# Row maxima of the scores from a 64-row product, two heads side by side, in an attention and feed-forward kernel

## The chip, the cores and the metric

The kernel runs on one core of one Trainium2 chip. The metric is device time in microseconds (us) of one execution; less is better. The kernel before was run three times. Its profile is of one further execution of the same program, recorded by the hardware.

## What is computed

Attention over 8 batches of 12 heads, 448 positions and a head width of 64, and then a feed-forward layer over the 3584 positions. All is in fp32 at the border of the kernel; the weights come as 64-bit floats.

```python
q_n, k_n = rmsnorm(q, g_q), rmsnorm(k, g_k)
scores = (q_n @ k_n.T) / sqrt(64)
scores = scores - max(scores, axis=-1)
attn = exp(scores); attn = attn / (sum(attn, axis=-1) + 1e-9)
x = heads side by side of attn @ v          # 3584 x 768
out = (s * relu(x @ w_in) ** 2 + b) @ w_out   # 768 -> 2048 -> 768
```

The maximum that is subtracted is only a shift: whatever is taken in its place comes out again in the division by the sum, as long as the exponentials neither overflow nor vanish.

## The kernel before

**Two parts.** The first part does the attention and, in its gaps, the first product of the feed-forward layer (`x @ w_in`) of the batch before. The second part does the last batch's first product and then `@ w_out`. Matmul operands are fp32r; where fp32r is not precise enough an operand is split into a high part and the rest, so that a product takes up to three matmuls.

**Pairs and slots.** Heads go in 48 pairs, j = 0 the even one and j = 1 the odd one. The program is a list written out slot by slot: 8 slots for a pair (`W`), one for each of four chunks of keys of each head, and 22 slots ahead of pair 0. Slot s of pair p stands at 8p + s; here "slot 0 to 7 of a pair" is meant. In a slot TensorE gets, in this order:

- `score_t` (L407, L410): two matmuls into the tile `st`, keys on the rows and queries along the columns. The first multiplies `ka` by `qa`, the second adds `kb` by `qb`.
- two matmuls `ph` of the feed-forward product as filling (L182),
- `score` (L369): one matmul into `sh`, with queries on the rows: a quarter of a head's queries (every fourth one, 112 columns of weights) against all 448 keys. It serves the maxima alone,
- two more `ph`, then `weigh` (L466): two or three matmuls `av`, weighting the values, for the slot before the last, and two more `ph`.

The filling starts at slot 60 of the list (`START`), in pair 7. In the first 12 pairs `weigh` is one fp32 matmul instead of the two or three.

**The tiles ka, qa, kb, qb** have 128 rows, 448 columns for each head of a pair, and exist twice (pairs take turns). For each head rows 0 to 63 of `ka` hold the high part of the keys and rows 64 to 127 the rest; `qa` holds the high part of the queries in both halves. So `ka` by `qa` over 128 rows gives k_hi q_hi + k_lo q_hi. `kb` holds the high part of the keys in rows 0 to 63 and a row of ones in row 64, `qb` the rest of the queries in rows 0 to 63 and in row 64 the negated maximum; the other rows are zero. So the exponent's argument is complete when both matmuls are done.

**How a head gets there.** Up to pair 8 (`NR` is 9) the heads come by `load_rows`, `norm_rows`, `turn` and `split_turned`; from pair 9 on by `load_kq`, `spread`, `scale` (POOL L331, VectorE L332, 15 slots ahead of the head's first slot), `split_kq` (ScalarE L350, L351 13 slots ahead, POOL L353, L354 one slot later) and `double_kb` (a DMA of `ka`'s high part to `kb`, 10 slots ahead).

**The maxima.** `score` of a product runs ten slots ahead of its number (`AHEAD`), so one in every slot. `maximum` (VectorE L380) follows in the same slot, and writes a column of `nmx`. When a head's four are there, `shift` (DMA on SP's queue, L357) writes them to the row of `qb`, six slots ahead of the head's first slot.

**Order on the other engines.** In a slot VectorE gets the slot's preparations (`ssq` L311, `scale` L332, `split_x` L516), then `split_e_lo` of the slot before (L447, the low part `al` of the exponentials), then `maximum`, then `convert` and `invert`. ScalarE gets `split_e` of the slot before (L434), `exponent` (L426 or L422), the slot's preparations, and `rectify` (L199). The low part `al` of a slot is thus made one slot later and used by `weigh` two slots later. Engines run in the order that is written; each takes its instructions one after another. `split_x` comes once in 48 slots, in three slots in a row (slots 3, 4 and 5 of a pair), with two VectorE operations each; `ssq` and the odd head's `scale` both fall in slot 5.

**PSUM** has eight banks that are handed out in the order in which they came free (`psum`): a new tile waits until the last reader of the tile before it in that bank is through.

Of the kernel before, what the change touches and what calls it, by code (L numbers as in the profile page):

```python
# [9 lines left out]
F32 = mybir.dt.float32  # L10
# [3 lines left out]
ALU = mybir.AluOpType  # L14
# [11 lines left out]
AHEAD = 10  # L26
# [11 lines left out]
def attention_then_relu2_ffn(  # L38
# [30 lines left out]
    V, S, G, T = nc.vector, nc.scalar, nc.gpsimd, nc.tensor  # L69

    NPAIR, P, _, SEQ = kq.shape
# [4 lines left out]
    D = P // 2  # L76
# [4 lines left out]
    NR = rows0.shape[0]  # L81
    NQ = 4
    QC = SEQ // NQ
# [9 lines left out]
    W = 8  # L93
# [18 lines left out]
    def psum(name):  # L112

        bank = free.pop(0)
        return ps.tile([P, 512], F32, tag=bank, name=name), bank
# [95 lines left out]
    with tc.tile_pool(name="apool", bufs=1) as ap:  # L211
# [40 lines left out]
        def split_turned(p, j):  # L252
            n, a = p % 2, slice(j * SEQ, (j + 1) * SEQ)
            (k, k_bank), (q, q_bank) = (tks.pop((p, j, t)) for t in range(2))
            S.copy(ka[n][:D, a], k)
            S.activation(qa[n][:D, a], q, AF.Copy, scale=gqk[:D])
            S.activation(qa[n][D:, a], q, AF.Copy, scale=gqk[:D])
            yield
            V.tensor_tensor(ka[n][D:, a], k, ka[n][:D, a].bitcast(F32), ALU.subtract)  # L259
            V.scalar_tensor_tensor(  # L260
                qb[n][:D, a], q, gqk[:D], qa[n][:D, a].bitcast(F32), ALU.mult, ALU.subtract
            )
            free.extend((k_bank, q_bank))

# [4 lines left out]
        def warm_up(n):  # L269

            to, bank = psum("warmth")
            for _ in range(n):
                T.matmul(to[:, :P], ident, ident, start=True, stop=True)
            free.append(bank)
# [58 lines left out]

        ka = [ap.tile([P, 2 * SEQ], F32R, name=f"ka{n}") for n in range(2)]
        qa = [ap.tile([P, 2 * SEQ], F32R, name=f"qa{n}") for n in range(2)]
        kb = [ap.tile([P, 2 * SEQ], F32R, name=f"kb{n}") for n in range(2)]
        qb = [ap.tile([P, 2 * SEQ], F32R, name=f"qb{n}") for n in range(2)]
        for t in qb:  # L340
            G.memset(t[D:P].bitcast(F32), 0.0)
        for t in kb:
            G.memset(t[D:P].bitcast(F32), 0.0)
            G.memset(t[D : D + 1].bitcast(F32), 1.0)

        def split_kq(p, j):

            t, n = kqs.pop((p, j)), p % 2
            a = slice(j * SEQ, (j + 1) * SEQ)
            S.copy(ka[n][:, a], t[:, 0])  # L350
            S.copy(qa[n][:, a], t[:, 1])  # L351
            yield
            G.tensor_tensor(ka[n][D:, a], t[D:, 0], ka[n][D:, a].bitcast(F32), ALU.subtract)  # L353
            G.tensor_tensor(qb[n][:D, a], t[:D, 1], qa[n][:D, a].bitcast(F32), ALU.subtract)  # L354

        def move(to, of):
            nc.sync.dma_start(to.bitcast(F32), of.bitcast(F32))  # L357

        def double_kb(p, j):
            a = slice(j * SEQ, (j + 1) * SEQ)  # L360
            move(kb[p % 2][:D, a], ka[p % 2][:D, a])

        def score(i):

            p, c = divmod(i, W)
            j, c = divmod(c, NQ)
            sh, bank = psum(f"sh{i}")
            a = slice(j * SEQ, (j + 1) * SEQ)
            T.matmul(  # L369
                sh[:QC, :SEQ], qa[p % 2][:, a].rearrange("k (p c) -> k c p", c=NQ)[:, c],  # L370
                ka[p % 2][:, a], start=True, stop=True,
            )
            shs[i] = sh, bank

        def maximum(i):
            p, c = divmod(i, W)
            if c == 0:
                nmxs[p] = ap.tile([QC, W], F32R, tag="nmx", bufs=2, name=f"nmx{p}")
            sh, bank = shs.pop(i)
            V.tensor_reduce(  # L380
                out=nmxs[p][:, c : c + 1], in_=sh[:QC, :SEQ], op=ALU.max, axis=AX.X, negate=True
            )
            free.append(bank)

        def shift(p, part):

            to = qb[p % 2][D : D + 1, part * SEQ : (part + 1) * SEQ]
            move(
                to.rearrange("o (p c) -> o p c", c=NQ), nmxs[p][:, part * NQ : (part + 1) * NQ]
            )  # L390
            if part:
                nmxs.pop(p)
# [35 lines left out]
        def split_e(i):  # L428
            p, j, kc, rows = chunk(i)
            if p < NV:  # L430
                return
            ah = ap.tile([P, SEQ], F32R, tag="ah", bufs=3, name=f"ah{i}")
            movers[i] = [ah]
            S.copy(ah[:rows], sts[i][0][:rows, :SEQ])  # L434
# [120 lines left out]
        def filler(n):  # L555

            for _ in islice(fill, n):
                pass
# [4 lines left out]
        def at(s_, f, *a):  # L563
            jobs[s_].append((f, a))

        for p in range(NPAIR):
            s0 = W * p
            if p >= NR:
                at(s0 - 32, load, p)
                at(s0 - 28, norm, p)  # L570
                at(s0 - 24, keep, p)
            for j in range(2):
                s1 = s0 + 4 * j
                if p >= NR:
                    at(s1 - 19, load_kq, p, j)
                    at(s1 - 19, spread, p, j)
                    at(s1 - 15, scale, p, j)
                    at(s1 - 13, split_kq, p, j)
                else:
                    at(max(s1 - 28, FIRST), load_rows, p, j)  # L580
                    at(s1 - 20, norm_rows, p, j)
                    at(s1 - 13, turn, p, j)
                    at(s1 - 12, split_turned, p, j)
                at(s1 - 10, double_kb, p, j)
                at(s1 - 6, shift, p, j)
                at(s1 + 6, take, p, j)
                at(s1 + 7, gather, p, j)
            at(s0 - (9 if p >= NV else 5), load_v, p)
            if p >= NV:
                at(s0 - 3, split_v, p)  # L590
            at(s0 + 13, invert, p)
            at(s0 + 14, divide, p, 1)
            at(s0 + 16, divide, p, 2)
            at(s0 + 18, divide, p, 3)
# [10 lines left out]
        def within(i):  # L605
            return 0 <= i < NSLOT
# [3 lines left out]
        gqk = cpool.tile([P, 1], F32, name="gqk")  # L610
        sb_s = cpool.tile([P, 1], F32, name="sb_s")
        sb_b = cpool.tile([P, 1], F32, name="sb_b")
        with tc.manual_schedule(engines=ORDERED):
            begun = []
            for s_ in range(FIRST, NSLOT + START + 1):
                if s_ == FIRST:
                    nc.sync.dma_start(gg, g_qk)
                    V.scalar_tensor_tensor(gqk, gg[:, 0:1], D**-0.5, gg[:, 1:2], ALU.mult, ALU.mult)
                if s_ == 0:
                    for t, x in ((sb_s, s), (sb_b, b_)):  # L620
                        nc.sync.dma_start(t, x.rearrange("(o d) -> o d", o=1).broadcast_to([P, 1]))
                if s_ == FIRST:
                    warm_up(30)
                if within(s_):
                    score_t(s_)
                filler(FILL[0])
                if within(s_ - 1):
                    split_e(s_ - 1)
                if within(s_):
                    exponent(s_)  # L630
                begun = [g for g in begun if next(g, 0) is None]
                keep_r()
                for f, a in jobs[s_]:
                    if f in late:
                        continue
                    g = f(*a)
                    if g is not None and next(g, 0) is None:
                        begun.append(g)
                ahead = s_ + AHEAD
                scored = within(ahead)  # L640
                if scored:
                    score(ahead)
                filler(FILL[1])
                rectify()
                if within(s_ - 1):
                    split_e_lo(s_ - 1)
                if scored:
                    maximum(ahead)
                for f, a in jobs[s_]:
                    if f in late:  # L650
                        f(*a)
                if within(s_ - 2):
                    weigh(s_ - 2)
                filler(FILL[2])
                b, m = divmod(s_ + 1 - START, W * NP)
                if m == 0 and b > 0:
                    filler(None)
                    units = [(b - 1, fc) for fc in range(NFC)]
                    fill = chain.from_iterable(ffn_in(xs, *u) for u in units) if b < B else iter(())
            rectify()  # L660
            keep_r()
# [146 lines left out]
```

## Time and profile before

| | us |
|---|---|
| median of three runs | 1484.6 |
| lowest and highest of them | 1483.02, 1485.44 |
| the profiled execution | 1483.03 |
| its span, first to last instruction | 1481.2 |
| first scoring matmul `st` starts (slot 0 of pair 0) | 27.0 |
| slot 4 of pair 7 (the filling starts) | 135.5 |
| slot 0 of pair 12 | 232.1 |
| last scoring matmul `st` | 933.1 |

The profiled execution stands 1.57 us under the median of the three runs and inside their spread. 1.83 us of it lie around the span.

How to read what follows. PE is TensorE's matmuls and PEld its weight loads, DVE is VectorE, ACT is ScalarE, POOL is GpSimd, SP the queue of DMA issues. A row of a timeline has the start in us, the duration in us, engine, line, operation, output tile and inputs, shapes, and how many instructions were merged into it (x2: two of them); in brackets idle time of the engine ahead of it and what ended it. For a matmul the shape `128*112 128x448` is rows times columns of the weights, then rows times columns of what streams past. A matmul's duration is modelled to its end, and runs beyond the start of the next one, so what a matmul costs is read from the distance of the starts. A row of windows has the stretch, its length, then for each engine its busy time and number of instructions, then the granted clock, the share of DMA and GB/s.

### The profile page before, as it was taken

The page shows a single profiled execution, that of the slowest core. Times are in us where ns is not written, and L with a number is a line of the kernel's source. Part 1 is how long each engine was busy: PE and PEld are TensorE (multiplying, and loading weights), DVE is VectorE, ACT ScalarE, POOL GpSimd, SP SyncE. Part 2 cuts the span into 40 slices and gives each one's busy share as a digit, 9 for nine tenths or more (in the row PEclk, how much of TensorE's full clock was granted, in tenths as well). Part 3 has the DMA queues.
Part 4 walks back from the last instruction along what each step waited for, and adds up shares of the span by engine and source line. Part 5 has one row for each costly group of instructions (what it writes and reads, how often), then busy time and mean ns, then how long its engine had stood idle before and what let it go on. Part 6 is the DMA issues. An engine that isn't in the chain of part 4 may idle for free. (4 is left out here: it accounts for less than half of the span.)

```text
span 1481.2 us, 21369 instructions
## 1 busy us (share of the span) xinstructions
PE 1443.3 (97%) x7332; PEld 1322.6 (89%) x7332; DVE 862.8 (58%) x1328; ACT 790.5 (53%) x1445; POOL 686.9 (46%) x563
## 2 busy tenths in 40 slices
PE   7998999999999999999999999999999999999998
PEld 6665788899899899899899889999999999999998
DVE  7999996766766666766766664389522222222210
ACT  5777556766766666766766766456322222222210
POOL 7788887777677777777677763100000000000000
PEclk8999999999999999999999999999999999999999
DMA  5456876566666666566666652387333333233200
GB/s 141 130 159 183 233 219 203 171 196 186 188 190 184 189 192 185 170 199 191 188 175 198 189 171 58 118 273 242 105 97 85 96 94 78 79 91 106 79 22 32
DMA packets 218172, 225.31 MB, mean 152 GB/s; under 512 B 77936, under 2 KB 195696, under 8 KB 218064
## 3 DMA queue, kind: packets, MB, share of 16 engines
q1 hardware_dynamic: 218064, 223.95, 51.7%
q8 instruction: 58, 0.95, 0.3%
q14 instruction: 50, 0.41, 0.1%
HBM read 171.71 MB, written 40.82 MB: 143 GB/s over the span
## 5 line engine op out<-in xcount | busy, mean ns | idle before, releaser
L182 PE MATMUL ph<-x,wih 128*128 128x448 f32 x1536 | 490.0, 366 | 1.8 <-DVE x L516 1.8
L182 PEld LDWEIGHTS ph<-x,wih 128*128 128x128 f32 x1536 | 288.7, 188 | 31.7 <-issue 6.4
L380 DVE TENSOR_REDUCE nmx<-sh 112x1 fp32r<-112x448 f32 x384 | 237.0, 620 | 130.7 <-PE sh L369 127.7
L182 PE MATMUL ph<-x,wil 128*128 128x448 f32 x768 | 293.8, 383 | 0.0
L426 ACT ACTIVATE st<-st 128x448 f32<-128x448 f32 (+1 forms) x288 | 151.2, 525 | 220.3 <-PE st L410 213.6
L707 PE MATMUL po<-woh,gh 128*128 128x384 f32 x896 | 228.1, 334 | 0.3 <-ACT r L199 0.3
L707 PE MATMUL po<-wol,gh 128*128 128x384 f32 x896 | 227.9, 334 | 0.0
L707 PE MATMUL po<-woh,gl 128*128 128x384 f32 x896 | 227.7, 334 | 0.0
L466 PE MATMUL av<-ah,vs 128*128 128x448 f32 x576 | 164.3, 366 | 0.1
L369 PE MATMUL sh<-ka,qa 128*112 128x448 f32 x384 | 147.3, 386 | 16.0 <-DVE ka L259 10.9
L707 PEld LDWEIGHTS po<-woh,gh 128*128 128x128 f32 x896 | 161.9, 188 | 0.7 <-ACT r L199 0.6
L707 PEld LDWEIGHTS po<-wol,gh 128*128 128x128 f32 x896 | 161.9, 188 | 0.0
L707 PEld LDWEIGHTS po<-woh,gl 128*128 128x128 f32 x896 | 161.7, 188 | 0.0
L407 PE MATMUL st<-qa,ka 128*128 128x448 f32 (+1 forms) x384 | 159.2, 415 | 1.7 <-ACT e L422 0.8
L182 PEld LDWEIGHTS ph<-x,wil 128*128 128x128 f32 x768 | 144.3, 188 | 17.8 <-issue 6.9
L434 ACT CAST ah<-st 128x448 fp32r<-128x448 f32 (+1 forms) x288 | 153.9, 534 | 1.8
L447 DVE TENSOR_TENSOR al<-st,ah 128x448 fp32r<-128x448 f32 x216 | 132.4, 613 | 35.4 <-ACT ah L434 21.6
L689 ACT ACTIVATE r<-r 128x2048 f32<-128x2048 f32 x28 | 53.7, 1919 | 172.7 <-DMA r<-r_d 172.7
L410 PE MATMUL st<-qb,kb 128*128 128x448 f32 (+1 forms) x384 | 140.2, 365 | 0.0
L690 DVE TENSOR_SCALAR r<-r,sb_s,sb_b 128x2048 f32<-128x2048 f32 x28 | 37.6, 1346 | 173.2 <-ACT r L689 173.2
L507 POOL TENSOR_TENSOR u<-uz,zb 64x448 f32<-64x448 f32 x96 | 115.4, 1203 | 41.4 <-DMA zb<-z_d 27.7
L369 PEld LDWEIGHTS sh<-ka,qa 128*112 128x112 f32 x384 | 107.5, 281 | 28.9 <-ACT wih L138 4.7
(75 smaller groups left out, 2142.1 us busy)
## 6 DMA issues: line engine op xcount, KB each, us to landing
kq<-in_dram SPq DMA_DIRECT2D x78, 448.0 KB, 4.9
rb<-i_d SPq DMA_DIRECT2D x78, 448.0 KB, 5.9
r_d<-r SPq DMA_DIRECT2D x128, 224.0 KB, 2.8
r<-r_d SPq DMA_DIRECT2D x24, 1024.0 KB, 5.9
raw<-in_dram SPq DMA_DIRECT2D x39, 448.0 KB, 5.1
w64i<-in_dram SPq DMA_DIRECT2D x24, 512.0 KB, 4.9
w64o<-in_dram SPq DMA_DIRECT2D x32, 384.0 KB, 4.7
kb<-ka SPq DMA_DIRECT2D x96, 112.0 KB, 3.1
```

Of the source, the lines that this page charges most:

```text
L182: T.matmul(ph[:, :SEQ], w[:, cc, f0 : f0 + P], xs[b, cc][:, part, :], start=n == 0, stop=n == 3 * NCC - 1,)
L369: T.matmul(sh[:QC, :SEQ], qa[p % 2][:, a].rearrange("k (p c) -> k c p", c=NQ)[:, c], ka[p % 2][:, a], start=True, stop=True,)
L380: V.tensor_reduce(out=nmxs[p][:, c : c + 1], in_=sh[:QC, :SEQ], op=ALU.max, axis=AX.X, negate=True)
L407: T.matmul(st[:rows, :SEQ], ka[n][:, keys], qa[n][:, q], start=True, stop=False)
L410: T.matmul(st[:rows, :SEQ], kb[n][:, keys], qb[n][:, q], start=False, stop=True,)
L426: S.activation(st[:rows, :SEQ], st[:rows, :SEQ], AF.Exp)
L434: S.copy(ah[:rows], sts[i][0][:rows, :SEQ])
L447: V.tensor_tensor(al, st[:rows, :SEQ], ah[:rows].bitcast(F32), ALU.subtract)
L466: T.matmul(av[:, :SEQ], x, a, start=kc == 0 and m == 0, stop=kc == 3 and m == len(todo) - 1,)
L507: G.tensor_tensor(u[a], uzs.pop((p, j))[a], zb[a], ALU.mult)
L689: S.activation(r, r, AF.Square)
L707: T.matmul(po[e][0][:, :HALF], x[:, fc, :], w[:, f, e * HALF : (e + 1) * HALF], start=fc == 0 and m == 0, stop=fc == NFC - 1 and m == 2,)
```

## The change

**From pair 9 on `score` uses 64 rows instead of 128**: the high part of the keys by the high part of the queries, without the product of the keys' rest. For the even head these are rows 0 to 63, for the odd head rows 64 to 127. So the layout of an odd head is turned over: its high part of the keys stands in rows 64 to 127 of `ka` and `kb`, its rest in rows 0 to 63, and the row of ones and the row of maxima is row 0 instead of 64. The list `half` says which rows are meant.

**From pair 9 on the products come in fours of slots**: in slots 0 to 3 of the pair before, each slot has the even head's product and right behind it the odd head's; slots 4 to 7 have none. Up to pair 8 all is as it was.

**The shift** of both heads is moved: from six slots ahead of each head's first slot (six and two slots ahead of the pair's slot 0) to four and three slots ahead of the pair's slot 0.

**At the start** each fill of `qb` and `kb` is done for each head apart, since the halves differ: 12 fills of 448 columns instead of 6 of 896.

```diff
+        half = [slice(0, D), slice(D, P)]
...
+        for j in range(2):
+            a, o = slice(j * SEQ, (j + 1) * SEQ), (1 - j) * D
+            for t in qb:
+                G.memset(t[half[1 - j], a].bitcast(F32), 0.0)
+            for t in kb:
+                G.memset(t[half[1 - j], a].bitcast(F32), 0.0)
+                G.memset(t[o : o + 1, a].bitcast(F32), 1.0)
...
-            G.tensor_tensor(ka[n][D:, a], t[D:, 0], ka[n][D:, a].bitcast(F32), ALU.subtract)
-            G.tensor_tensor(qb[n][:D, a], t[:D, 1], qa[n][:D, a].bitcast(F32), ALU.subtract)
+            h, o = half[j], half[1 - j]
+            G.tensor_tensor(ka[n][o, a], t[o, 0], ka[n][o, a].bitcast(F32), ALU.subtract)
+            G.tensor_tensor(qb[n][h, a], t[h, 1], qa[n][h, a].bitcast(F32), ALU.subtract)
...
-            move(kb[p % 2][:D, a], ka[p % 2][:D, a])
+            move(kb[p % 2][half[j], a], ka[p % 2][half[j], a])
...
-                sh[:QC, :SEQ], qa[p % 2][:, a].rearrange("k (p c) -> k c p", c=NQ)[:, c],
-                ka[p % 2][:, a], start=True, stop=True,
+                sh[:QC, :SEQ], qa[p % 2][rows, a].rearrange("k (p c) -> k c p", c=NQ)[:, c],
+                ka[p % 2][rows, a], start=True, stop=True,
...
+        def to_score(s_):
+            p, c = divmod(s_ + AHEAD, W)
+            if 0 <= p < NR:
+                yield W * p + c, slice(0, P)
+            p, c = divmod(s_ + W, W)
+            if NR <= p < NPAIR and c < NQ:
+                for j in range(2):
+                    yield W * p + NQ * j + c, half[j]
...
-                at(s1 - 6, shift, p, j)
+                at(s1 - 6 if p < NR else s0 - 4 + j, shift, p, j)
...
-                if scored:
-                    maximum(ahead)
+                for i, _ in scored:
+                    maximum(i)
```

`split_turned` has its rows exchanged in the same way for odd heads. No operation but the fills changes in number or size.

**TensorE's order.** The slot of `st200` (slot 0 of pair 25) before, from its first scoring matmul to its last; names carry the number of the tile and of its buffer:

```order
L407 MATMUL st200_5529<-qa1_187,ka1_185 128x448
L410 MATMUL st200_5529<-qb1_191,kb1_189 128x448
L182 MATMUL ph2_14_5504<-x2_2_4300,wih3_1931 128x448
L182 MATMUL ph2_14_5504<-x2_2_4300,wil3_1932 128x448
L369 MATMUL sh210_5546<-ka0_184,qa0_186 112x448
L182 MATMUL ph2_14_5504<-x2_2_4300,wih3_1931 128x448
L182 MATMUL ph2_14_5504<-x2_3_4303,wih3_1931 128x448
L466 MATMUL av24_1_5495<-ah198_5507,vs0_2530 128x448 x2
L466 MATMUL av24_1_5495<-al198_5521,vs0_2530 128x448
```

The same slot now:

```order
L424 MATMUL st200_5528<-qa1_187,ka1_185 128x448
L427 MATMUL st200_5528<-qb1_191,kb1_189 128x448
L182 MATMUL ph2_14_5506<-x2_2_4312,wih3_1937 128x448
L182 MATMUL ph2_14_5506<-x2_2_4312,wil3_1938 128x448
L374 MATMUL sh208_5545<-ka0_184,qa0_186 112x448
L374 MATMUL sh212_5547<-ka0_184,qa0_186 112x448
L182 MATMUL ph2_14_5506<-x2_2_4312,wih3_1937 128x448
L182 MATMUL ph2_14_5506<-x2_3_4315,wih3_1937 128x448
L483 MATMUL av24_1_5497<-ah198_5509,vs0_2540 128x448 x2
L483 MATMUL av24_1_5497<-al198_5521,vs0_2540 128x448
```

Where one product `sh210` stood, there are the even head's first (`sh208`) and the odd head's first (`sh212`), in two banks, with nothing between them; ahead of them and behind them stand matmuls over 128 rows, as before.

**VectorE's order.** From the maximum of that slot on, before:

```order
L380 TENSOR_REDUCE nmx26_5493<-sh210_5546 112x1
L332 SCALAR_TENSOR_TENSOR kq27_0_5453<-kq27_0_5453,gqk_200,rb27_0_5455 128x448
L447 TENSOR_TENSOR al200_5575<-st200_5529,ah200_5562 128x448
L380 TENSOR_REDUCE nmx26_5493<-sh211_5571 112x1
L447 TENSOR_TENSOR al201_5604<-st201_5557,ah201_5588 128x448
L380 TENSOR_REDUCE nmx26_5493<-sh212_5598 112x1
```

and now:

```order
L396 TENSOR_REDUCE nmx26_5552<-sh208_5545 112x1
L396 TENSOR_REDUCE nmx26_5552<-sh212_5547 112x1
L332 SCALAR_TENSOR_TENSOR kq27_0_5463<-kq27_0_5463,gqk_206,rb27_0_5465 128x448
L464 TENSOR_TENSOR al200_5580<-st200_5528,ah200_5565 128x448
L396 TENSOR_REDUCE nmx26_5552<-sh209_5574 112x1
L396 TENSOR_REDUCE nmx26_5552<-sh213_5576 112x1
L464 TENSOR_TENSOR al201_5611<-st201_5560,ah201_5594 128x448
```

In slots 0 to 3 two maxima stand between one low part `al` and the next, in slots 4 to 7 none.

**SP's order.** The shift of pair 26's even head (`qb0<-nmx26`) and what stands around it, before:

```order
L327 DMA rb27_1_5569<-i_d27_157 128x2x448
L357 DMA qb0_190<-nmx26_5493 1x112x4
L357 DMA kb0_188<-ka0_184 64x448
L209 DMA r_d2_76<-r2_14_5602 128x448
L483 DMA zt24_5484<-uz24_1_5594 64x1x7
L267 DMA kq28_0_5686<-in_0_dram 128x2x448
```

and now:

```order
L361 DMA kb0_188<-ka0_184 64x448
L209 DMA r_d2_76<-r2_14_5609 128x448
L500 DMA zt24_5491<-uz24_1_5600 64x1x7
L361 DMA qb0_190<-nmx26_5552 1x112x4 x2
L267 DMA kq28_0_5696<-in_0_dram 128x2x448
L327 DMA rb28_0_5698<-i_d28_158 128x2x448
```

Both heads' shifts now stand together. The even head's has moved behind the copy to `kb0`, the store of `r2_14` and the gathering of the sums `zt24`; the odd head's, which stood two rows behind a store and `z_d24` further on, has moved ahead of the loads of `kq28` and `rb28`.

More of the change, by code (lines that the diff above doesn't have):

```diff
@@ L254, in split_turned @@
             (k, k_bank), (q, q_bank) = (tks.pop((p, j, t)) for t in range(2))
-            S.copy(ka[n][:D, a], k)
+            S.copy(ka[n][half[j], a], k)
             S.activation(qa[n][:D, a], q, AF.Copy, scale=gqk[:D])
@@ L258, in split_turned @@
             yield
-            V.tensor_tensor(ka[n][D:, a], k, ka[n][:D, a].bitcast(F32), ALU.subtract)
+            V.tensor_tensor(ka[n][half[1 - j], a], k, ka[n][half[j], a].bitcast(F32), ALU.subtract)
             V.scalar_tensor_tensor(
-                qb[n][:D, a], q, gqk[:D], qa[n][:D, a].bitcast(F32), ALU.mult, ALU.subtract
+                qb[n][half[j], a], q, gqk[:D], qa[n][:D, a].bitcast(F32), ALU.mult, ALU.subtract
             )
@@ L339, in attention_then_relu2_ffn @@
         qb = [ap.tile([P, 2 * SEQ], F32R, name=f"qb{n}") for n in range(2)]
[L340 to L344, printed above, removed]
+        for j in range(2):
[5 more added lines that the diff above has]
+                G.memset(t[o : o + 1, a].bitcast(F32), 1.0)
         def split_kq(p, j):
@@ L360, in double_kb, with score @@
             a = slice(j * SEQ, (j + 1) * SEQ)
-            move(kb[p % 2][:D, a], ka[p % 2][:D, a])
-        def score(i):
+            move(kb[p % 2][half[j], a], ka[p % 2][half[j], a])
+        def score(i, rows=slice(0, P)):
             p, c = divmod(i, W)
@@ L385, in shift @@
         def shift(p, part):
-            to = qb[p % 2][D : D + 1, part * SEQ : (part + 1) * SEQ]
+            o = (1 - part) * D
+            to = qb[p % 2][o : o + 1, part * SEQ : (part + 1) * SEQ]
             move(
@@ L638, in attention_then_relu2_ffn @@
                         begun.append(g)
-                ahead = s_ + AHEAD
-                scored = within(ahead)
-                if scored:
-                    score(ahead)
+                scored = list(to_score(s_))
+                for i, rows in scored:
+                    score(i, rows)
                 filler(FILL[1])
@@ L646, in attention_then_relu2_ffn @@
                     split_e_lo(s_ - 1)
-                if scored:
-                    maximum(ahead)
+                for i, _ in scored:
+                    maximum(i)
                 for f, a in jobs[s_]:
```

## The prediction

> **What bounds the kernel now.** First the page: the head and the engines' shares.
>
> ```profile
> span 1481.2 us, 21369 instructions
> PE 1443.3 (97%) x7332; PEld 1322.6 (89%) x7332; DVE 862.8 (58%) x1328; ACT 790.5 (53%) x1445; POOL 686.9 (46%) x563
> ```
>
> TensorE is busy nearly all the time, but that is a mean over stages. So next the windows, by stage: the last part of the fp32 pairs, then pairs 13 to 46, then one ordinary pair and one in which a batch ends.
>
> ```profile
> 135.50:232.00 96.50, 93.50 (x392) 74.03 (x391) 86.32 (x110) 56.16 (x110) 85.77 (x70) 1.00 0.78 230
> 252.00:900.00 648.00, 636.88 (x3106) 579.60 (x3105) 441.07 (x728) 447.52 (x916) 467.69 (x361) 1.00 0.63 184
> 350.50:369.60 19.10, 19.10 (x96) 17.55 (x95) 12.37 (x21) 13.18 (x27) 14.09 (x12) 1.00 0.65 185
> 369.60:391.50 21.90, 20.05 (x96) 17.50 (x95) 16.96 (x28) 15.57 (x33) 15.46 (x12) 1.00 0.56 169
> ```
>
> In an ordinary pair TensorE is busy all 19.10 us; VectorE, ScalarE and GpSimd work 12 to 14 of them. Only where a batch ends does TensorE stand, 1.85 us. The view of waits for this stage names one thing that TensorE waits for:
>
> ```profile
> PE av L466 <- DVE al L447: 9.1, 10, 1.0
> ```
>
> So in this stage the end is set by how long TensorE takes for its list. The timeline of TensorE over one slot, from scoring matmul to scoring matmul, gives the price of one entry:
>
> ```profile
> 534.49 0.37 PE L182 MATMUL ph<-x,wih 128*128 128x448 f32 x1
> 534.70 0.36 PE L407 MATMUL st<-qa,ka 128*64 128x448 f32 x1
> 534.90 0.36 PE L410 MATMUL st<-qb,kb 128*64 128x448 f32 x1
> 535.10 0.37 PE L182 MATMUL ph<-x,wih 128*128 128x448 f32 x1
> 535.30 0.37 PE L182 MATMUL ph<-x,wil 128*128 128x448 f32 x1
> 535.51 0.36 PE L369 MATMUL sh<-ka,qa 128*112 128x448 f32 x1
> 535.71 0.57 PE L182 MATMUL ph<-x,wih 128*128 128x448 f32 x2
> ...
> 537.14 0.36 PE L407 MATMUL st<-qa,ka 128*128 128x448 f32 x1
> ```
>
> Twelve matmuls stand from 534.70 to 537.14 (two scoring ones, two `ph`, `sh`, two `ph`, and five behind them): 2.44 / 12 = 0.203 us each. `sh` is no exception: 535.51 to 535.71. Eight of them make 1.6 us of each pair.
>
> In the fp32 pairs the slot is longer:
>
> ```profile
> 180.06 0.36 PE L407 MATMUL st<-qa,ka 128*128 128x448 f32 x1
> ...
> 182.63 0.36 PE L407 MATMUL st<-qa,ka 128*128 128x448 f32 x1
> ```
>
> 2.57 us, although fewer matmuls are in it; eight such slots make 20.6. TensorE has its list to do there too, but VectorE works 86.32 of 96.50 us and stands close behind.
>
> **The change part by part.**
>
> *What goes from TensorE's list.* Pairs 9 to 47 are 39; each has eight products, which become four side by side. If both of a slot run at the same time, one place of 0.203 us goes in each of 39 x 4 = 156 slots: 156 x 0.203 = 31.7 us.
>
> *What two side by side cost more than one.* The profile of before has no product on half the rows, so I bound it. Rows of the loads and of the products, grouped, for the long stage:
>
> ```profile
> L369 PE MATMUL sh<-ka,qa 128*112 128x448 f32 x246 | 89.9, 366 | 0.0
> L369 PEld LDWEIGHTS sh<-ka,qa 128*112 128x112 f32 x246 | 68.9, 280 | 4.3
> L182 PEld LDWEIGHTS ph<-x,wih 128*128 128x128 f32 x982 | 184.7, 188 | 14.8
> ```
>
> The load of a product's weights (every fourth column) takes 280 ns and not 188, yet costs nothing today, since it lies under the matmul ahead. From below: nothing, if both loads lie there together; it can't be a gain beyond the 0.203, since one product stays. From above: the second load begins only when the first product starts, so the second product comes a whole place later, 0.203, or, if all 280 ns are then waited for, 0.280. The nearest row for a change of form is the scoring pair `128*64` at 534.70: into it and out of it the starts lie 0.21, 0.20 and 0.20 apart, as anywhere. That row changes columns and not rows, but it is the only switch of the array's shape in the steady stage, and it is free. I take 0.02 a slot, near it: 156 x 0.02 = 3.1 us given back.
>
> Of two products on separate rows the Trainium skill ("TensorE: Matmul & The Clock Gate", Part 3, "The mechanism") says that they run at once, with starts some 4 ns apart. No run here shows it. By that page the cost would be 156 x 0.004 = 0.6 us instead of 3.1, an estimate, and the forecast 2.5 us lower.
>
> *VectorE's two maxima in a slot.* The timeline of VectorE in slot 5 of a pair:
>
> ```profile
> 520.01 1.09 DVE L311 TENSOR_REDUCE ssq<-raw 128x14 f32<-128x896 f32 x1 [0.18 <-ACT raw L306]
> 521.02 0.68 DVE L332 SCALAR_TENSOR_TENSOR kq<-kq,gqk,rb 128x448 f32<-128x448 f32 x1
> 521.61 0.62 DVE L447 TENSOR_TENSOR al<-st,ah 128x448 fp32r<-128x448 f32 x1
> 522.14 0.61 DVE L380 TENSOR_REDUCE nmx<-sh 112x1 fp32r<-112x448 f32 x1
> 522.68 0.89 DVE L489 TENSOR_SCALAR zt<-zt 128x7 f32<-128x7 f32 x1
> ```
>
> By the starts, `ssq` takes 1.0, `scale` 0.6, `al` and a maximum 0.53 each. Slots 0 to 3 now hold one `al` and two maxima, 1.6 us, and slot 1 the `scale` too, 2.2, under 2.44. Slot 5, which holds 2.67 today, loses its maximum. So VectorE keeps up, and the wait for `al` doesn't grow in ordinary pairs. A product's bank now was in use one slot before, where mostly two slots lay between. From a product's start to the next slot's are 2.44 us; less 0.37 for the product and 1.06 for two maxima, 1.0 us is left. I cost that at nothing; it is gone when VectorE runs half a slot late, and TensorE then waits for a bank.
>
> At a batch's end VectorE is behind already. What stands ahead of the `al` that is waited for stays the same (two maxima move ahead of it by a slot or two, none goes), but TensorE arrives up to two places of 0.2 sooner. So up to 0.4 us goes back to waiting at each of the six ends from pair 13 on: 2.0 us.
>
> In the fp32 pairs VectorE's share is 89%. Pairs 9 to 12 make their products there, 16 slots; I take half of their 3.2 us: 1.6 given back (between none and all).
>
> *When the products' inputs are there.* An odd head's first product now stands one slot behind the `split_kq` that makes its operands, where it stood three slots behind it:
>
> ```profile
> 536.20 0.56 ACT L351 CAST qa<-kq 128x448 fp32r<-128x448 f32 x1
> 537.95 0.37 PE L369 MATMUL sh<-ka,qa 128*112 128x448 f32 x1
> ```
>
> ScalarE has the copy ready at 536.76, in the slot ahead; the product of the next slot starts at 537.95 and its load 0.2 sooner. That slot ahead is now 0.2 shorter. About 0.8 us are left, so it costs nothing; if not, 39 waits (below). GpSimd's half of the split isn't read by the products any more: one wait less.
>
> *The shift.* The even head's goes two slots later, and on SP's queue behind a copy, a store and a gathering.
>
> ```profile
> 513.23 0.63 SPq L357 DMA_DIRECT2D qb<-nmx  x1
> 527.77 0.36 PE L410 MATMUL st<-qb,kb 128*128 128x448 f32 x1
> DMA to landing us min/median/max: 1.9/3.2/7.4
> ```
>
> Today it is issued 14.5 us ahead of the matmul that reads it and lands after 7.4 at most. Two slots are 4.9 us: 9.6 are left, 2.2 above the slowest. The odd head's gains a slot. Nothing on SP's queue waits long behind them, since the maxima are those of the slot before. No cost.
>
> *The fills at the start.* GpSimd's timeline:
>
> ```profile
> 0.24 0.10 POOL L777 MEMSET const-float32-0.0<- 128x1 f32 x1 [0.24 <-issue]
> 1.03 0.84 POOL L341 MEMSET qb<- 64x896 f32 x1
> 6.38 0.20 POOL L238 TENSOR_SCALAR ri<-ssq 112x8 f32<-112x8 f32 x1
> ```
>
> The six fills stand right ahead of the first head's `ri`. Six more instructions for the same elements cost between nothing and 0.1 each (a fill of one column, in the first row, takes that): half of 0.6, 0.3 us, if the start goes straight through to the end.
>
> *The sum.* 31.7 - 3.1 - 2.0 - 1.6 - 0.3 = 24.7 us. The profiled execution's 1483.03 becomes 1458.3. It stands 1.6 under the median of the three runs, 1484.6, from which it would be 1459.9. I forecast 1459.
>
> **The rivals.**
>
> *One after the other.* The second load can't go ahead of the first product, and the second product starts when the first ends. For it speaks that in every row of the timeline each load waits for one matmul to begin; against it, that nothing ever stood there on other rows. Then the 156 slots gain nothing, and nothing is lost at the batch ends, as TensorE isn't faster: 1484.6 + 0.3 = 1485, and 1497 if the 280 ns are paid (156 x 0.077 = 12). Chance 0.14. The change would then not do what it says.
>
> *Emptying the array at each switch (slower).* If a product on 64 rows can't start before all matmuls on 128 rows are through, and the next `ph` not before the products are, each slot pays twice the time that a matmul runs on beyond the next one's start: 366 - 203 = 163 ns. Twice that, 326, less the 203 gained, is 0.123 x 156 = 19.2 us: 1503. It decides from 0.10 us a switch on. If the loads can't go ahead either, 188 ns for the `ph` behind come on top: 156 x 0.188 = 29 more, 1533. The row `128*64` at 534.70 speaks against it. Chance 0.16. This is the rule of the Trainium skill ("TensorEngine Tiling (Array Packing)", Tiling Modes, "Key Properties"): changing the tiling mode, and not just the tile, drains the engine. The trace doesn't bear it out for a change in columns, with 0.20 us on both sides; for a change in rows no run here shows it.
>
> *Late data eats a part.* The odd head's first product waits for `qa`, or the bursts on VectorE hold a bank: 39 pairs x 0.3 us = 12 us back, 1471. For it: the slack of 0.8 us is an ordinary pair's, and ScalarE and VectorE are later where a batch ends. Against: both have idle time in each ordinary pair. Chance 0.08.
>
> **How the numbers follow.** The forecast's chance is 0.62; its own range goes from 1453 (1484.6 less all of the 31.7) to 1469 (a slot pays 0.077 for the longer load, 12 us instead of 3.1). The whole range takes in late data and the plain case of one after the other, and at both ends the 2.4 us by which the three runs differ: 1450 to 1489; out of it lie the emptying and the end of the serial case that pays 280 ns. What a measurement can tell from no change is about 0.2%, 3 us. Faster: the forecast, late data and a little of the serial case, 0.72. Same: most of the serial case, 0.10. Slower: the emptying and the rest, 0.18.
>
> **What the profile after would show.** Right: two `sh` starting within some 0.03 us of each other on TensorE, the next `ph` 0.2 behind; an ordinary pair at about 18.4 us instead of 19.1; the wait of `av` for `al` near 11 us; no wait of `sh` for ScalarE. Wrong: starts of the two `sh` 0.2 or more apart (serial); a gap ahead of the first `sh` and behind the second (emptying); waits of `sh` for `qa` or for `nmx` (late data).

## The result and the profile after

The changed kernel takes 1534.6 us (median of four runs, 1533.87 to 1536.46) against 1484.6 us before: ratio 1.034, 95% interval 1.0322 to 1.0358. It is 50 us slower. The forecast was 1459, faster, with a range up to 1489; the rival in which TensorE is emptied at each switch, with the loads in the open, had been worked out at 1533.

The page of the changed kernel, head and engines:

```profile
span 1533.6 us, 21411 instructions
PE 1488.2 (97%) x7332; PEld 1289.7 (84%) x7332; DVE 865.2 (56%) x1328; ACT 791.3 (52%) x1445; POOL 668.6 (44%) x569
```

TensorE still counts as busy for 97%, with the same 7332 matmuls, although 156 places of its list were to go. Only the weight loads, PEld, show that something is wrong: their share fell from 89 to 84%. The windows of the long stage, of an ordinary pair (pair 20) and of the pair before it, in which a batch ends:

```profile
252.00:900.00 648.00, 632.15 (x2912) 517.21 (x2912) 424.68 (x682) 420.49 (x859) 421.06 (x341) 1.00 0.61 175
406.86:427.14 20.28, 20.28 (x96) 16.75 (x94) 13.10 (x21) 13.22 (x28) 12.38 (x11) 1.00 0.64 184
382.79:406.86 24.07, 21.05 (x96) 16.51 (x94) 17.06 (x27) 16.03 (x34) 15.41 (x13) 1.00 0.55 156
```

Where 3106 matmuls fitted into 648 us there are 2912. An ordinary pair takes 20.28 us instead of 19.15 with TensorE busy throughout, at the full granted clock of 1.00; the other engines have more idle time than before. So nobody is waited for there: the list itself takes longer. (That the busy time has no hole is the model of the matmuls' ends: a record runs on beyond the next one's start.) Where a batch ends TensorE stands for 3.02 us, against 1.85 before.

TensorE's timeline over one slot with two products, first the matmuls:

```profile
407.26 0.36 PE L182 MATMUL ph<-x,wih 128*128 128x448 f32 x1
407.46 0.36 PE L182 MATMUL ph<-x,wil 128*128 128x448 f32 x1
407.75 0.56 PE L374 MATMUL sh<-ka,qa 64*112 64x448 f32 x2
408.25 0.67 PE L182 MATMUL ph<-x,wih 128*128 128x448 f32 x2
408.76 0.57 PE L483 MATMUL av<-ah,vs 128*128 128x448 f32 x2
```

and the weight loads of the same stretch:

```profile
407.06 0.19 PEld L182 LDWEIGHTS ph<-x,wih 128*128 128x128 f32 x1
407.27 0.19 PEld L182 LDWEIGHTS ph<-x,wil 128*128 128x128 f32 x1
407.75 0.28 PEld L374 LDWEIGHTS sh<-ka,qa 64*112 64x112 f32 x2 [0.30 <-issue]
408.25 0.30 PEld L182 LDWEIGHTS ph<-x,wih 128*128 128x128 f32 x2 [0.21 <-issue]
408.56 0.39 PEld L483 LDWEIGHTS av<-ah,vs 128*128 128x128 f32 x2
```

Three things are to be seen.

- **The two products do run at once.** Merged, the two `sh` take 0.56 and their two loads 0.28, the length of a single one each; their records start 3 to 4 ns apart.
- **A load ordinarily starts with the matmul ahead of it** (407.27 with the `ph` of 407.26). The products' loads start at 407.75, 0.29 behind the `ph` of 407.46. So they wait out that matmul's place of 0.203 and 0.09 more, and then lie in the open, with no matmul running over them: the record of the products runs 0.56, 0.20 longer than a matmul's 0.36, so they begin in effect at 407.95.
- **The same happens on the way back.** The next `ph`'s load starts at 408.25, 0.30 behind 407.95 (a place and 0.10), and again nothing is under way while it runs: the second `ph` is started at 408.56, where the next load begins, one place behind the first, which so began in effect at 408.35.

From the `ph` of 407.46 to the second `ph` behind at 408.56 are 1.10 us. Three places would be 0.61. So the two switches cost 0.49 us a slot, of which 0.09 and 0.10 are emptying and 0.20 and 0.10 loads in the open. (The 0.49 and the first 0.29 come from recorded starts; the split of the rest rests on the two effective starts, which are worked out.) Against this stands one place of 0.203 gained. The net, 0.28 in 156 slots, is 44 us.

That is what the pairs show. Slot 0 of two pairs that follow each other, before:

```profile
410.07 0.36 PE L407 MATMUL st<-qa,ka 128*128 128x448 f32 x1
429.22 0.36 PE L407 MATMUL st<-qa,ka 128*128 128x448 f32 x1
```

and after:

```profile
406.86 0.36 PE L424 MATMUL st<-qa,ka 128*128 128x448 f32 x1
427.14 0.36 PE L424 MATMUL st<-qa,ka 128*128 128x448 f32 x1
```

19.15 became 20.28: 1.13 in a pair, 0.28 for each of its four slots, 39 x 1.13 = 44 us. The batch ends give the rest. A pair with a batch end took 21.76 (2.61 more than an ordinary one), and now takes 24.07 (3.79 more): six times 1.18 is 7. 44 + 7 = 51, where the medians differ by 50. The waits of TensorE in the long stage, 250 to 850 us, after (us in total, times, longest):

```profile
PE av L483 <- DVE al L464: 11.3, 10, 1.5
PE av L483 <- ACT x L532: 3.8, 5, 0.8
```

These are the batch ends. Each has three waits now, of 0.74, 0.76 and 1.52 us; before it had two, of 0.96 and 0.86. Rows around the second and the third:

```profile
398.93 0.62 DVE L464 TENSOR_TENSOR ah<-st,ah 64x448 fp32r<-64x448 f32 x1
399.69 0.64 PE L483 MATMUL av<-ah,vs 128*128 128x448 f32 x2 [0.76 <-ACT x L532]
400.58 1.65 DVE L332 SCALAR_TENSOR_TENSOR kq<-kq,gqk,rb 128x448 f32<-128x448 f32 x1
403.90 0.47 PE L483 MATMUL av<-al,vs 128*128 128x448 f32 x1 [1.52 <-DVE al L464]
```

The second is put down to ScalarE's copy of `x`, but this `av` reads no `x`. It reads `ah`, whose last part (the low part of the chunk with 64 keys, kept in the free rows of `ah`) VectorE has ready at 399.55. So all three waits are for low parts that VectorE makes. No product waits for its operands or its bank, and no scoring matmul for the row of maxima.

### The profile page after: what moved, and what is told of

Read it like the earlier page. It is cut to its first block, busy times and chain, and to the rows that moved or that the text cites. A ratio compares the mean times of both kernels' runs of the same rounds, so it can differ in the third digit from the quotient of the medians.

```text
span 1533.6 us, 21411 instructions
## 1 busy us (share of the span) xinstructions
PE 1488.2 (97%) x7332; PEld 1289.7 (84%) x7332; DVE 865.2 (56%) x1328; ACT 791.3 (52%) x1445; POOL 668.6 (44%) x569
## 5 line engine op out<-in xcount | busy, mean ns | idle before, releaser
L182 PE MATMUL ph<-x,wih 128*128 128x448 f32 x1536 | 505.8, 376 | 3.0 <-DVE x L533 2.9
L182 PEld LDWEIGHTS ph<-x,wih 128*128 128x128 f32 x1536 | 276.2, 188 | 67.8 <-issue 39.8
L396 DVE TENSOR_REDUCE nmx<-sh 112x1 fp32r<-112x448 f32 x384 | 223.4, 618 | 120.6 <-PE sh L374 120.2
L357 POOL TENSOR_TENSOR ka<-kq,ka 64x448 fp32r<-64x448 f32 x78 | 90.2, 1156 | 139.8 <-ACT ka L353 139.5
L374 PE MATMUL sh<-ka,qa 64*112 64x448 f32 (+1 forms) x384 | 121.8, 545 | 15.0 <-DVE ka L259 6.0
```

Source lines behind the costliest of these rows:

```text
L182: T.matmul(ph[:, :SEQ], w[:, cc, f0 : f0 + P], xs[b, cc][:, part, :], start=n == 0, stop=n == 3 * NCC - 1,)
L357: G.tensor_tensor(ka[n][o, a], t[o, 0], ka[n][o, a].bitcast(F32), ALU.subtract)
L374: T.matmul(sh[:QC, :SEQ], qa[p % 2][rows, a].rearrange("k (p c) -> k c p", c=NQ)[:, c], ka[p % 2][rows, a], start=True, stop=True,)
L396: V.tensor_reduce(out=nmxs[p][:, c : c + 1], in_=sh[:QC, :SEQ], op=ALU.max, axis=AX.X, negate=True)
```

## Experiments

Theory 1 was that each change between products on 64 and matmuls on 128 rows empties TensorE and puts a load in the open. Theory 2 was the order: two maxima in a row, banks taken again sooner. Theory 3 was that a product on 64 rows is itself slow. The kernel before was run beside each group, at 1484.0, 1484.4 and 1484.8 us.

**The order without the form.** The changed kernel, its products on 128 rows; its row maxima are not those of the scores.

```diff
-                sh[:QC, :SEQ], qa[p % 2][rows, a].rearrange("k (p c) -> k c p", c=NQ)[:, c],
-                ka[p % 2][rows, a], start=True, stop=True,
+                sh[:QC, :SEQ], qa[p % 2][:, a].rearrange("k (p c) -> k c p", c=NQ)[:, c],
+                (qa if p >= NR else ka)[p % 2][:, a], start=True, stop=True,
```

> The changed kernel's order (two products in slots 0 to 3, none in 4 to 7, its shift and layout) with the products of pairs 9 on made on 128 rows instead of 64. It streams qa in place of ka, so that nothing new is waited for; the row maxima are then not those of the scores, which is left out on purpose. Theory 1, emptying (each change between products on 64 and on 128 rows empties TensorE and puts a weight load in the open): no such change is left, so the time of before, 1484.6, up to 7 us more if the batch ends (24.07 us in the changed kernel, 21.76 before) owe their loss to the order. Theory 2, the order (bursts on VectorE, banks taken again after one slot): the loss stays, about 1530. Theory 3, a product on 64 rows is itself slow: 1484.6 as well.

Measured: 1492.2 us, 1.0053 of before (1.0037 to 1.0069). Ordinary pairs are back at 19.17, pairs with a batch end take 23.2, 4.05 more. So the form makes some 42 of the 50 us, and the order makes 8, all of it at the batch ends (six times 1.44 is 8.6). Theory 2 is right for that part alone.

**One product on 64 rows in each slot.** The kernel before, in its own order.

```diff
             sh, bank = psum(f"sh{i}")
+            rows = slice(0, P if p < NR else D)
...
-                sh[:QC, :SEQ], qa[p % 2][:, a].rearrange("k (p c) -> k c p", c=NQ)[:, c],
-                ka[p % 2][:, a], start=True, stop=True,
+                sh[:QC, :SEQ], qa[p % 2][rows, a].rearrange("k (p c) -> k c p", c=NQ)[:, c],
+                ka[p % 2][rows, a], start=True, stop=True,
```

> The kernel before in its own order and layout, one product in each slot, but from pair 9 on on rows 0 to 63 (the product with the keys' rest is left out of the maxima, as in the changed kernel). Theory 1, emptying: 312 slots instead of 156 pay the two changes, each the 0.887 us that the changed kernel's trace shows from the last ph before to the effective start of the ph behind, less the 0.406 that two places take: 312 x 0.481 = 150, so 1635; somewhat less where VectorE sets the pace. Theory 2, the order: 1484.6, since it is the order of before. Theory 3, slow products: half of the 0.683 us that a slot's two take, 0.341 less a place of 0.203, times 312 = 43, so 1528.

Measured: 1619.3 us, 1.0912 (1.0895 to 1.0928). An ordinary pair takes 22.96, 3.81 more: 0.476 a slot in eight slots, where 0.481 was expected. The timeline of its matmuls around one product:

```profile
406.25 0.36 PE L182 MATMUL ph<-x,wil 128*128 128x448 f32 x1
406.54 0.56 PE L370 MATMUL sh<-ka,qa 64*112 64x448 f32 x1
407.03 0.68 PE L182 MATMUL ph<-x,wih 128*128 128x448 f32 x2
407.55 0.57 PE L467 MATMUL av<-ah,vs 128*128 128x448 f32 x2
```

One product shows the same 0.29 ahead of it, the same 0.56, and the same 0.49 to the next `ph` as the two together. So the price isn't paid per product, and theory 3, with 1528, is out; a slow product whose slowness two at once share is still open here, and the next run settles it. The whole came out 16 us under the 1635, 11 of them because the six batch ends from pair 13 on cost only 0.7 each instead of 2.6: TensorE is so slow that it waits for `al` only once at each, for 0.15 us.

**Both products on the same rows.** The layout of before for both heads, in the changed order.

```diff
-                    yield W * p + NQ * j + c, half[j]
+                    yield W * p + NQ * j + c, half[0]
...
-            S.copy(ka[n][half[j], a], k)
+            S.copy(ka[n][half[0], a], k)
...
-            h, o = half[j], half[1 - j]
+            h, o = half[0], half[1]
...
-            move(kb[p % 2][half[j], a], ka[p % 2][half[j], a])
+            move(kb[p % 2][half[0], a], ka[p % 2][half[0], a])
...
-            o = (1 - part) * D
+            o = D
```

> The changed kernel's order with both heads' products on rows 0 to 63 (the layout of before for both), so that the two of a slot can't run at once; no change of form stands between them. Theory 1, emptying, with real concurrency of the two in the changed kernel: one place more in 156 slots, 156 x 0.203 = 31.7, so 1566. If the two in the changed kernel ran one after the other (their starts in the records only seeming equal): no difference, 1534.6.

Measured: 1564.8 us, 1.054 (1.0521 to 1.0558), 30 us above the changed kernel. The two products in its timeline:

```profile
415.58 0.36 PE L182 MATMUL ph<-x,wil 128*128 128x448 f32 x1
415.88 0.77 PE L374 MATMUL sh<-ka,qa 64*112 64x448 f32 x2
416.57 0.67 PE L182 MATMUL ph<-x,wih 128*128 128x448 f32 x2
```

0.77 instead of 0.56, and 0.69 instead of 0.50 to the next `ph`: one place more. So the two of the changed kernel truly run at once, and the gain that was forecast, a place in each of 156 slots, is there.

The run shows one thing more. The second product, on 64 rows right behind another on 64 rows, costs just a place, so a product on 64 rows isn't slow in itself. An ordinary pair takes 21.11, 1.96 more than before with the same eight products: 0.49 for each of its four slots. One product, two at once and two in a row thus pay the same 0.48 to 0.49 for going in and out.

**Weights side by side.** The changed kernel with 112 neighbouring columns as weights; it streams `qa` too, and its row maxima are not those of the scores.

```diff
+            of = "k (p c) -> k c p" if p < NR else "k (c p) -> k c p"
...
-                sh[:QC, :SEQ], qa[p % 2][rows, a].rearrange("k (p c) -> k c p", c=NQ)[:, c],
-                ka[p % 2][rows, a], start=True, stop=True,
+                sh[:QC, :SEQ], qa[p % 2][rows, a].rearrange(of, c=NQ)[:, c],
+                (ka if p < NR else qa)[p % 2][rows, a], start=True, stop=True,
```

> The changed kernel with the products' weights taken as 112 columns that lie side by side instead of every fourth one, from pair 9 on, and qa streamed in place of ka (the row maxima are then not those of the scores and go to other queries: left out on purpose). The load of every fourth column takes 276 ns in the records and 196 of them pass before the product's effective start; a load of columns side by side (188 ns, ph) shows 104 before its matmul's effective start when it lies in the open. Theory 1 with the load in the open: 156 x (0.196 - 0.104) = 14 less, about 1520. If only the emptying counts and the loads lie under it: 1534.6, as changed.

Measured: 1516.5 us, 1.0214 (1.0198 to 1.0229), 18 us less than the changed kernel. Its loads:

```profile
407.56 0.17 PEld L375 LDWEIGHTS sh<-qa 64*112 64x112 f32 x2 [0.31 <-issue]
407.95 0.30 PEld L182 LDWEIGHTS ph<-x,wih 128*128 128x128 f32 x2 [0.22 <-issue]
```

The load takes 0.17 instead of 0.28, and the next one comes 0.39 behind it instead of 0.50. An ordinary pair is 0.49 shorter (19.79), 0.12 a slot. Streaming `qa` has no part in that: the run on 128 rows streamed it as well, at before's 19.17 a pair. The length of this load had no price before, when it lay under a matmul; in the open the 0.11 us by which it got shorter come back whole. Even so the slot stays dearer than two places.

**96 rows.** As the single products, with 96 rows instead of 64.

```diff
-            rows = slice(0, P if p < NR else D)
+            rows = slice(0, P if p < NR else 96)
```

> As the run with single products on 64 rows in the order of before, but on rows 0 to 95 from pair 9 on (the maxima take half of the product with the keys' rest; the other half is left out). Such a product needs no half of the array to itself. Theory 1, the price belongs to the form for half the rows: 1484, as before, where 64 rows gave 1619. Rival, any product on fewer than 128 rows pays: about 1619.

Measured: 1484.4 us, 1.0004 (0.9994 to 1.0013), no change. Grouped rows of its products:

```profile
L370 PE MATMUL sh<-ka,qa 96*112 96x448 f32 x245 | 91.2, 372 | 0.0
L370 PEld LDWEIGHTS sh<-ka,qa 96*112 96x112 f32 x246 | 68.8, 280 | 3.9
```

96 rows cost nothing; 64 rows do.

**The batch ends: maxima moved away.** The 8 us of the order were still to be explained. My theory was crowding on VectorE in slots 3 to 5. The kernel before, its products (128 rows) from pair 9 on two to a slot in slots 6, 7, 1 and 2; the norm one slot later; and both.

```diff
+            for j, at_ in ((0, 10), (1, 7)):
+                p, c = divmod(s_ + at_, W)
+                if NR <= p < NPAIR and c < 2:
+                    for m in range(2):
+                        yield W * p + NQ * j + 2 * c + m
...
-                at(s0 - 28, norm, p)
+                at(s0 - 27, norm, p)
```

> The kernel before, with products on all 128 rows and its layout, but from pair 9 on the products go two to a slot into slots that are free of the batch end's work: the even head's into slots 6 and 7, the odd head's into slots 1 and 2. Theory, crowding (the batch end's 2.6 us are VectorE's work in slots 3 to 5, where the splits of x, ssq and scale meet maxima): VectorE then has 6.4 us there against TensorE's 6.7, so most of 2.6 us goes at each of seven ends: 1466 to 1475. Rival, ScalarE (the copies of x on ScalarE are late, and the maxima don't matter): 1484, and the 8 us that the four-slot order cost on 128 rows then come from elsewhere.

> The kernel before with the norm of a pair one slot later (ssq in slot 6 instead of 5), all else as before. Crowding: slot 5 loses 1.0 us of VectorE's work, so about 1 us goes at each of seven ends: 1477. Rival, ScalarE: 1484, or up to 3 us less, since the square on ScalarE moves from slot 4 to 5 as well.

> Both moves: products away from slots 3 to 5 and the norm one slot later. Crowding: as the first alone or up to 3 us less, 1464 to 1473. Rival, ScalarE: 1481 to 1484.

Measured: 1497.8 (1.0094, 1.008 to 1.0108), 1503.5 (1.0135, 1.0121 to 1.0149) and 1495.5 us (1.0078, 1.0065 to 1.0091): all slower, and the batch ends longer (23.1 and 24.6, 22.8 and 24.4, 22.8, against 21.76). Crowding, which had them shorter, falls. VectorE at a batch end of the first of them:

```profile
503.57 2.23 DVE L526 TENSOR_TENSOR x<-u,x 128x448 fp32r<-128x448 f32 x2 [2.90 <-ACT x L525]
505.72 0.61 DVE L457 TENSOR_TENSOR al<-st,ah 128x448 fp32r<-128x448 f32 x1
```

and TensorE's wait behind it:

```profile
506.38 0.47 PE L476 MATMUL av<-al,vs 128*128 128x448 f32 x1 [1.42 <-DVE al L457]
```

VectorE isn't crowded at that point. It stands idle for 2.90 us until ScalarE has copied `x`, then splits it for 2.2 us, and only then makes the `al` that TensorE needs. Maxima have no part in it. The kernel before has the same at each of its batch ends, and a second wait 6 us later:

```profile
378.87 2.24 DVE L516 TENSOR_TENSOR x<-u,x 128x448 fp32r<-128x448 f32 x2 [3.17 <-ACT x L515]
381.03 0.61 DVE L447 TENSOR_TENSOR al<-st,ah 128x448 fp32r<-128x448 f32 x1
381.70 0.47 PE L466 MATMUL av<-al,vs 128*128 128x448 f32 x1 [0.96 <-DVE al L447]
385.44 0.68 DVE L332 SCALAR_TENSOR_TENSOR kq<-kq,gqk,rb 128x448 f32<-128x448 f32 x1
387.77 0.47 PE L466 MATMUL av<-al,vs 128*128 128x448 f32 x1 [0.86 <-DVE al L447]
```

Up to the second wait VectorE works without a pause; ahead of that `al` stand `ssq`, `scale` and two more splits. Moving the products made the first wait longer, 1.42 instead of 0.96: two products (0.41 us) fewer lie between slot 3's `st`, behind which ScalarE gets to `x`, and the `av` of slot 4 that waits.

Part of the loss of these runs is the granted clock. It was 0.50 for 3.41 us behind three of the six batch ends of the first run and three of the second, and these are the ends that took 24.6 and 24.4 us. In the first run, such a stretch and one behind an end of 23.1 us:

```profile
274.85:278.26 3.41, 3.41 (x11) 2.80 (x10) 2.86 (x7) 1.89 (x4) 2.35 (x2) 0.50 0.27 51
395.00:398.41 3.41, 3.41 (x18) 3.05 (x18) 3.38 (x7) 1.89 (x4) 2.74 (x3) 1.00 0.26 43
```

11 matmuls instead of 18. Of the norm's move, 10 us had come by pair 12 already, with two more such stretches among them (at 158.0 and 229.7). In the profile of before the clock is full from 25 us to the end. The ends at the full clock are longer than 21.76 as well, so crowding falls without these stretches too. What brings such a stretch on, and the rest of the three losses, isn't settled.

**The batch ends: the splits behind al.** So the splits of `x` were moved to the end of the slot, behind `al` and the maxima: in the kernel before, and in the changed one.

```diff
                 S.copy(x[:, 0, :], u)
-                V.tensor_tensor(x[:, 1, :], u, x[:, 0, :].bitcast(F32), ALU.subtract)
+                us[b * NP + g] = u
+
+        def split_x_lo(b, k):
+            for g in (2 * k, 2 * k + 1):
+                u, x = us.pop(b * NP + g), xs[b, g]
+                V.tensor_tensor(x[:, 1, :], u, x[:, 0, :].bitcast(F32), ALU.subtract)
...
-        late = (convert, invert)
+        late = (convert, invert, split_x_lo)
...
+                at(W * NP * (b + 1) + START - 2 + k_, split_x_lo, b, k_)
```

> The kernel before, with VectorE's two splits of x per slot at the end of the slot, behind al and the maximum, instead of ahead of them. In the run with the products moved away from the batch end, TensorE's wait for al stayed (1.4 us at the end that was looked at, 0.96 before): VectorE's queue holds al behind two splits of x, which wait for ScalarE's copies. Theory, queued behind: with al ahead of the splits the batch end's 2.6 us fall by 1 us or more at seven ends: 1466 to 1478. Rival, the splits are needed as early as they stand: the next ph then wait for x, and it stays at 1484 or goes above.

> The changed kernel with the same edit. Queued behind: its batch ends cost 3.8 us each (24.07 less 20.28) and fall by 1 us or more: 1510 to 1528. If the ends' additional loss is the maxima standing two in a row, which this edit leaves: 1525 to 1528. Rival: 1534 or above. The emptying stays in every case: ordinary pairs at 20.3 us.

Measured: 1472.5 us, 0.9918 of before (0.9903 to 0.9933), and 1519.0 us, 1.0228 (1.0211 to 1.0245). Pairs with a batch end take 19.85 instead of 21.76 and, all but the first, 21.4 instead of 24.07. TensorE's wait in the long stage, in the first (before: 9.1, 10 times, 1.0 at the longest):

```profile
PE av L466 <- DVE al L447: 2.4, 6, 0.4
```

Most of the wait was the order of VectorE's queue: that of 0.96 is gone, and 0.40 is left of the 0.86. In the changed kernel one wait of 0.73 is left of the three. This version of the kernel before beats both kernels of this case, by 12 us and by 62. In the changed kernel the same edit takes off 16 us, and the ordinary pairs stay at 20.28: the form's price is independent of it.

## Why the prediction was wrong

- **What fell: "What two side by side cost more than one", taken at 0.02 us a slot.** It measured 0.49, for emptying at both switches and two loads in the open. The step took its price from the nearest row that changes the array's shape, the scoring pair `128*64`, whose switch is free. But that row changes the columns in use, and the products change the rows, and what holds for the one doesn't hold for the other. Its upper bound (0.280, a serial load) was too low as well: it let the load start with the first product at the latest, and had no term for the matmul ahead and the one behind.
- **What held of it: "one place of 0.203 us goes".** The products run at once; taking that away again cost 30 us, where 31.7 were worked out.
- **The rival that came.** Emptying at each switch, chance 0.16, 1503, or 1533 with the load of `ph` in the open. The mechanism is shown by the 0.29 and 0.30 in the loads' starts and by the same price for one product, two at once and two in a row. Its terms were not right one by one: emptying is 0.09 and 0.10 instead of 0.163 a switch, and two loads lie in the open, 0.20 and 0.10, instead of one of 0.188. Together that is 0.49 where the rival had 0.51, so part of the agreement is chance. The batch ends, which the rival left out, give another 7 us. With the Trainium skill's rule that a change of tiling mode drains the engine ("TensorEngine Tiling (Array Packing)", Tiling Modes, "Key Properties") the trace agrees for rows, with some 0.09 us a switch; for the scoring pair with 64 columns, with starts 0.20 apart, no draining shows.
- **The batch ends** were put at up to 0.4 us each, 2.0 in all, for TensorE coming sooner. They cost 1.44 each in the changed order on 128 rows, and 1.18 here. That what stands ahead of the awaited `al` stays the same was wrong in two places. Two maxima instead of one now stand between the first `al` and the low part of the 64-key chunk, which starts 2.76 us behind that `al` instead of 2.22; TensorE's slot there is a place of 0.20 shorter; together that is 0.74, about the new wait of 0.76. And `scale` ahead of the last `al` takes 1.65 instead of 0.68 (why isn't shown), with a wait of 1.52 instead of 0.86. That VectorE is behind with its work was only half of it: it starts late because its queue holds `al` behind splits that wait for ScalarE, 2.88 us at these ends.
- **The rest held or can't be told.** The products' `qa`, the banks and the shift wait nowhere in the long stage. Pairs 10 and 11 in the fp32 stage got longer by 1.1 like the others (20.5 to 21.68), so TensorE's list sets the pace there when it grows; whether a shorter list would have paid in full there wasn't seen. The first `st` starts at 26.2 to 28.3 us in runs of programs with the same fills, too wide a spread to see 0.3. The range's upper end, 1489, is higher than its own working: 1485 and 2.4 make 1487.
- **The chances.** I gave a free switch 0.62 on the strength of one row of another kind. No row of before had a product on half the rows, and the Trainium skill's rule of draining ("TensorEngine Tiling (Array Packing)", Tiling Modes, "Key Properties"), cited with that rival, spoke of any change of tiling mode. A price for which no row of the same kind exists should have left the two cases nearer to even.

## What to carry to other kernels

Work on half the array's rows pays only if the stretch between two switches is long: here a stretch costs 0.49 us for going in and out, and each pair of products in it gains 0.203. By these two figures it would take three pairs in a row to gain, an estimate that no run tried. A gain of that sort is to be priced per switch, with both loads in the open. TensorE's busy share doesn't show it; the distance from a matmul's start to the next load's start does.

When a matmul waits for an engine that has idle time, look at what stands ahead of the awaited instruction in that engine's queue, and what that waits for; moving the maxima and the norm away didn't help here, and moving the awaited instruction forward gave 12 us.

## What the runs showed of the hardware

- Two products on rows 0 to 63 and 64 to 127 start and load at the same time: two take the 0.56 us of one, on the same rows 0.77.
- Going from 128 rows to 64 and back costs 0.48 to 0.49 us, whether one product, two at once or two in a row lie between: some 0.09 us of standing each way, and no load goes ahead over the switch. 96 rows (1484.4 us), and 64 columns on 128 rows (starts 0.20 apart), cost nothing.
- A load of every fourth column takes 0.28 us and of neighbouring columns 0.17; this shows in the time when the load lies in the open (18 us here); under a matmul the 0.28 cost nothing.
- Where the granted clock was 0.50 for 3.41 us, 11 matmuls ran instead of 18, and a pair with a batch end took 1.5 us longer.
